# Seven-product form for half of the columns of a first matrix layer, and feature work given to either of two engines, in a fused attention and gated-layer kernel

## The chip, the cores and the metric

The kernel runs on one core of a Trainium2 chip. A core has five engines that run their own instruction streams beside each other: TensorE multiplies matrices (in the profile PE for the products and PEld for the loading of the stationary operand), VectorE (DVE) and ScalarE (ACT) do elementwise work, GpSimd (POOL) does small copies and issues some transfers, and SyncE (SP) issues the other transfers. An engine takes its instructions in the order in which they stand. The metric is the time of one execution in microseconds of device time; smaller is better. For the kernel before, the median of 11 runs is 292.11 us (291.77 to 294.96).

## What is computed

Two stages, one after the other, in float32 at the borders:

```python
# q, k, v: [8 batches, 8 heads, 576 positions, 64]
def phi(x, c, s):
    r = np.maximum(x, 0.0)
    return np.concatenate([r * c, r * s], axis=-1)
q_p, k_p = phi(q, cos_w, sin_w), phi(k, cos_w, sin_w)
kv  = np.einsum('bhsf,bhsd->bhfd', k_p, v)
num = np.einsum('bhsf,bhfd->bhsd', q_p, kv)
den = np.einsum('bhsf,bhf->bhs', q_p, k_p.sum(axis=2))[..., None] + 1e-06
x = (num / den).transpose(0, 2, 1, 3).reshape(4608, 512)
h = x @ w_in                  # w_in: [512, 2048]
g = h * np.cos(h)
out = g @ w_out               # w_out: [2048, 512], out: [4608, 512]
```

cos_w and sin_w depend on the position alone.

## The kernel before

The 4608 tokens are worked in nine chunks of 512. Chunks 0 to 7 are the first 512 positions of the eight batches; the last chunk (8) collects the 64 positions left over from each batch (tile xR in place of xT). Operands of the products are 16-bit floats, sums in PSUM are 32-bit.

**Attention of a batch.** Queries, keys and values are loaded in 32 bits into the tiles qm, km, vm. There is one such tile per name, so the next batch's load waits for the work that reads the present one. `prep` (lines 337 to 351) makes one of the two feature halves (cosine or sine) for one block of 128 tokens: relu and a scale per token, 128x512 values, written as 16 bits to kp or qp. `cast_v` (353 to 363) turns a block of v into 16 bits. From batch 2 on, `attention` (799 to 823) gives cosine halves and v casts to VectorE and sine halves to ScalarE. `kv` (365) multiplies keys and values on TensorE; `q_dma` and `x_dma` turn blocks round by transfers; `num` (419) makes numerator and denominator and has VectorE divide: an add, a reciprocal and a product (lines 450 to 454).

**First layer.** `layer1` (501 to 542) takes one chunk. From chunk 2 on it does 16 column blocks of 128, each as four products 128x128 by 128x512 that add up in one PSUM bank (line 539). Three banks M1 are used in turn. `gate` (491 to 499) then has ScalarE compute the cosine of the bank into a tile ch (as a sine with an offset, line 494) and VectorE multiply bank and ch into gT in 16 bits (line 496).

**Second layer.** From chunk 1 on `layer2` (609 to 693) splits g and w_out into 2x2 blocks and forms the four block results from seven block products in place of eight. The sums of blocks that this needs are made by VectorE: those of w_out once (`w_out_sums`, tiles T1 to T4, lines 595 to 607), those of g for each chunk (tiles S2, S3 and parts of gT in place, lines 625 and 670). Each product has two parts of eight matmuls 128x128 by 128x256 (line 643) in two banks M2 that go on adding while ScalarE (`copy`, 654) and VectorE (`plus`, 658) take out the running values into Y1, U2, Z5 and the output tiles ost.

**Order.** No loop sets the order of the instructions. Every call adds a step with an engine, a cost, a due time and the data that it reads and writes to a list (class `Plan`). `Plan.run` lays the list out by a forward pass (each engine takes the ready step with the smallest key) and a backward pass (which makes latest start times, the keys of the next forward pass), twelve times, and keeps the shortest. The instructions of every engine are then written in that order. So a change of one step's cost, engine or data can move others anywhere in the kernel.

Of the kernel before, what the change touches and what calls it, by code (L numbers as in the profile page):

```python
# [15 lines left out]

class Plan:


# [20 lines left out]
    def add(self, eng, occ, lat, due, fn, rd=(), wr=(), dma=None, lane=None):  # L40

        n = len(self.steps)
        prev = self.lanes.get(lane)
        if lane is not None:
            self.lanes[lane] = n
        deps = set()
        for key in rd:
            if key in self.wr:
                deps.add(self.wr[key])
        for key in wr:  # L50
            if key in self.wr:
                deps.add(self.wr[key])
            deps.update(self.rd.get(key, ()))
        for key in rd:
            self.rd.setdefault(key, []).append(n)
        for key in wr:
            self.wr[key] = n
            self.rd[key] = []
        deps.discard(n)
        self.steps.append(dict(eng=eng, occ=occ, lat=lat, due=due, fn=fn,  # L60
                               deps=deps, dma=dma, n=n, prev=prev))
        return n

    def run(self):


        key = [s["due"] for s in self.steps]
        best = None
        for _ in range(self.PASSES):
            start, done = self.forward(key)  # L70
            end = max(done)
            if best is None or end < best[0]:
                best = (end, start, done)
            key = self.backward(start, done, end)
        for s, a, b in zip(self.steps, best[1], best[2]):
            s["start"], s["end"] = a, b
        return sorted(self.steps, key=lambda s: (s["start"], s["n"]))

    def link(self, n, u):
        st = self.steps  # L80
        same = st[u]["eng"] == st[n]["eng"] and st[n]["dma"] is None
        return 0.0 if same else self.LINK[st[n]["eng"]]

    def forward(self, key):
# [9 lines left out]
        free = {e: 0.0 for e in self.LINK}  # L94
        ready = {e: [] for e in self.LINK}
        rings, now = {r: [] for r in self.SHARE}, 0.0
        for n, k in enumerate(left):
            if not k:
                ready[st[n]["eng"]].append(n)

        def release(n):
            for u in users[n]:
                avail[u] = max(avail[u], done[n] + self.link(n, u))
                left[u] -= 1
                if not left[u]:
                    ready[st[u]["eng"]].append(u)
        todo = len(st)
        while todo:
            best = None
            for e, cand in ready.items():  # L110
                if not cand:
                    continue
                limit = max(free[e], min(avail[n] for n in cand)) + self.PATIENCE.get(e, 0.0)
                k, t, n = min((key[n], max(free[e], avail[n]), n) for n in cand
                              if avail[n] <= limit)
                if best is None or t < best[0]:
                    best = (t, e, n)
# [23 lines left out]
            s = st[n]  # L141
            ready[e].remove(n)
            start[n] = t
            free[e] = t + s["occ"]
            if n in follow:
                u = follow[n]
                avail[u] = max(avail[u], t)
                left[u] -= 1
                if not left[u]:
                    ready[st[u]["eng"]].append(u)  # L150
            if s["dma"] is None:
# [53 lines left out]
def kernel(  # L205
# [41 lines left out]
    def sb(name, shape, dt=F16):  # L247
        return pool.tile(shape, dt, name=name)
# [4 lines left out]
    WARM = sb("WARM", [P, 1], F32)  # L253
    WZ = sb("WZ", [P, SM])
    w_in_sb = sb("w_in_sb", [P, NCT, Dff])
    w_out_sb = sb("w_out_sb", [P, NJT, Dm])
    V1 = sb("V1", [P, NT + 1, H, D1])
    JH, MH, TH = NJT // 2, Dm // 2, SM // 2
    T1, T2, T3, T4 = [sb(f"T{n}", [P, JH, MH]) for n in range(1, 5)]
    S2, S3 = [sb(f"S{n}", [P, JH, TH]) for n in (2, 3)]  # L260
    Y1, U2, Z5 = [sb(nm, [P, 2, MH], F32) for nm in ("Y1", "U2", "Z5")]
    raw = {nm: sb(f"{nm}m", [P, H, NT + 1, D], F32) for nm in "kqv"}
# [27 lines left out]

    Q_PE, X_PE = (), range(1, 3)
    ORDER0, ORDER1, HOLDW = "qkv", "kqv", 1
    GATE1 = (w_in_sb[0:2, 0, Dff // 2 + 1:Dff // 2 + 2], [("w_in", 2)])
# [14 lines left out]
    def act(occ, due, fn, rd, wr, lat=0.15):  # L308
        pl.add("ACT", occ, occ + lat, due, fn, rd, wr)


# [25 lines left out]
    def prep(b, nm, t, g, eng, due, hs=slice(0, H), after=()):  # L337
        dst = (kp if nm == "k" else qp)
        out_, in_ = dst[:, t, hs, g, :], raw[nm][:, hs, t, :]
        sc = CS[:, b % 2, g, t:t + 1]  # L340
        heads = range(H)[hs]
        rd = hk(nm, heads) + ["CS", *after]
        wr = [(nm + "p", t, g, h) for h in heads]
        f = len(heads) / H
        if eng == "ACT":
            act(0.12 + 0.5 * f, due, lambda: nc.scalar.activation(  # L346
                out=out_, in_=in_, func=AF.Relu, scale=sc), rd, wr)
        else:
            dve(0.09 + 0.33 * f, due, lambda: nc.vector.tensor_scalar(  # L349
                out=out_, in0=in_, scalar1=0.0, scalar2=sc,  # L350
                op0=ALU.max, op1=ALU.mult), rd, wr)

    def cast_v(b, t, eng, due, hs=slice(0, H)):
# [3 lines left out]
        f = len(heads) / H  # L357
        if eng == "ACT":
            act(0.12 + 0.5 * f, due, lambda: nc.scalar.activation(  # L359
                out=out_, in_=in_, func=AF.Copy), rd, wr)  # L360
        else:
            dve(0.09 + 0.33 * f, due, lambda: nc.vector.tensor_copy(  # L362
                out=out_, in_=in_), rd, wr)

# [136 lines left out]
    def layer1(c):  # L501
# [3 lines left out]
        if c < 2:  # L505
# [24 lines left out]
            return  # L530
        for n in range(NJT):
            j = n // 2 + (n % 2) * JH if c < B else n
            m = m1n[0] % NM1
            m1n[0] += 1
            due = start[c] + n * width[c] / NJT

            def mm(m=m, j=j):
                for cc in range(NCT):
                    nc.tensor.matmul(M1[m], lhsT=w_in_sb[:, cc, j * P:(j + 1) * P], rhs=X[:, cc, :],  # L539
                                     start=(cc == 0), stop=(cc == NCT - 1))  # L540
            pe(NCT, MM, due, mm, xk + [("w_in", j // 4)], [("M1", m)])
            gate(M1[m], ("M1", m), G[:, j, :], [("g", c % 2, j, t) for t in range(NT)], due + 1.5)

# [51 lines left out]
    def w_out_sums():  # L595
# [5 lines left out]
        def tt(out_, a, b, op, rd, wr):  # L601
            dve(1.14, start[2] - 8, lambda: nc.vector.tensor_tensor(
                out=out_, in0=a, in1=b, op=op), rd, wr)
        tt(T1, b12, b11, ALU.subtract, wk, ["T1"])
        tt(T3, b22, b12, ALU.subtract, wk, ["T3"])
        tt(T2, b22, T1, ALU.subtract, wk + ["T1"], ["T2"])
        tt(T4, b21, T2, ALU.subtract, wk + ["T2"], ["T4"])

    def layer2(c):
# [46 lines left out]

        def plus(dst, bank, other, ok, dk, due):
            dve(0.61, due, lambda: nc.vector.tensor_tensor(
                out=dst, in0=view(bank), in1=other, op=ALU.add), [("M2", bank), ok], dk)
        ol, oh = on[0] % NO, (on[0] + 1) % NO  # L660
        on[0] += 2
        m0, m1 = slice(0, MH), slice(MH, Dm)
        d = product(A, a11, W[:, lo, m0], gk(0, 0) + wk, True, False)
        copy(Y1, A, ["Y1"], d + 0.5)
        d = product(Bk, a12, W[:, hi, m0], gk(1, 0) + wk, True, True)
        plus(ost[ol][:, :, m0], Bk, Y1, "Y1", [("ost", ol, 0)], d + 0.5)
        for q_ in range(NG):
# [5 lines left out]
        d = product(A, S2, T2, sk["S2"] + ["T2"], False, False)  # L673
        copy(U2, A, ["U2"], d + 0.5)
        d = product(Bk, a21, T1, gk(0, 1) + ["T1"], True, False)
        copy(Z5, Bk, ["Z5"], d + 0.5)
        d = product(A, S3, T3, sk["S3"] + ["T3"], False, False)
        plus(ost[oh][:, :, m1], A, Z5, "Z5", [("ost", oh, 1)], d + 0.5)
        d = product(Bk, a12, W[:, hi, m1], gk(1, 0) + wk, False, True)
        plus(ost[ol][:, :, m1], Bk, U2, "U2", [("ost", ol, 1)], d + 0.5)  # L680
        store(c, 0, ol, d + 1.5)
# [14 lines left out]
    def setup():  # L696
        nc.gpsimd.memset(WZ, 0.5)
        nc.vector.memset(PIH, math.pi / 2.0)
# [100 lines left out]
    def attention(b):  # L799
# [3 lines left out]
        for t in range(NT + 1):  # L803
            for g in range(2):
                prep(b, "k", t, g, "DVE" if g == 0 else "ACT", T + 1.2 * t)
        for t in range(NT + 1):
            cast_v(b, t, "DVE", T + 6 + 0.4 * t)
        kv(b, T + 8)
        for t in range(NT + 1):
            due = T + 8 + 1.2 * t  # L810
            for g in range(2):
                prep(b, "q", t, g, "DVE" if g == 0 else "ACT", due)
            if b in Q_PE:
# [23 lines left out]
    for c in range(2, NC):  # L837
        if c < B:
            attention(c)
        layer2(c - 1)  # L840
        layer1(c)
# [36 lines left out]
```

## Time and profile before

| what | value |
|---|---|
| median of 11 runs | 292.11 us |
| profiled execution, own time | 293.9 us |
| its span, first to last instruction | 292.1 us |
| mean granted TensorE clock | 0.982 |
| PE busy | 278.6 us, 95% |
| PEld busy | 195.5 us, 67% |
| DVE busy | 239.4 us, 82% |
| ACT busy | 182.9 us, 63% |
| POOL busy | 8.7 us, 3% |
| HBM traffic over the span | 158 GB/s |

Busy is the time in which at least one instruction of an engine is on record. Instructions of one engine overlap at their ends: two gate products of VectorE that last 0.68 us each take 1.28 us together, so that a queue of them moves on every 0.60 us. The work of an engine in a stretch is therefore counted here by such steps from start to start. Waits are put down to the engine whose signal came last.

### The profile page before, as it was taken

What the parts mean: (1) busy time and instruction counts of PE and PEld (TensorE: products, weight loads), DVE (VectorE), ACT (ScalarE), POOL (GpSimd) and SP (SyncE); (2) the same over time, 40 slices, a digit from 0 to 9 for tenths busy, and PEclk for the clock granted to TensorE, in tenths of its full rate; (3) what the DMA queues carried; (4) which work ended last, traced back from release to release, by engine and by line L of the source; (5) the groups of instructions that cost most, each with busy time, mean ns of one, the idle gap of its engine ahead of it and who ended that gap; (6) DMA issues with size and microseconds to landing.
All of it is one profiled execution on the core that took longest, in us unless ns stands there. A gap on an engine that the chain in (4) does not pass through costs nothing.

```text
span 292.1 us, 6281 instructions
## 1 busy us (share of the span) xinstructions
PE 278.6 (95%) x2460; PEld 195.5 (67%) x2460; DVE 239.4 (82%) x486; ACT 182.9 (63%) x293; POOL 8.7 (3%) x21
## 2 busy tenths in 40 slices
PE   7768998999999999998999999999999999999993
PEld 2446866587976677566756766675668566666783
DVE  2965788999999999999998999999789948665741
ACT  2943899799967865867396759485543554645420
POOL 1502200000000000000000000000000000000000
PEclk9985999999999999999999999999999999999999
DMA  6999999799819996998899899944915000300304
GB/s 217 309 209 268 295 259 333 232 209 268 257 18 302 188 307 190 261 246 218 256 203 285 218 269 156 268 123 106 147 39 180 20 0 2 144 2 1 134 12 144
DMA packets 77565, 53.27 MB, mean 182 GB/s; under 512 B 46048, under 2 KB 75232, under 8 KB 77536
## 3 DMA queue, kind: packets, MB, share of 16 engines
q1 hardware_dynamic: 72592, 48.12, 63.2%
q0 software_dynamic: 4224, 4.19, 8.7%
q10 hardware_dynamic: 720, 0.57, 0.6%
q8 instruction: 19, 0.31, 0.4%
q14 instruction: 10, 0.08, 0.1%
HBM read 36.74 MB, written 9.44 MB: 158 GB/s over the span
## 4 chain that ended last, share of the span: by engine, by line
PE 84%; DMA 6%; ACT 5%; DVE 2%; issue 1%; POOL 0%; SPq 0%; ACTq 0%
PE M L643 33%; PE M L539 33%; PE M L521 9%; DMA w_in_sb<-in_moe_w_in_dram 3%; PE ATT L434 3%; DMA km<-in_k_dram 3%; PE ATT L373 2%; PE M L583 2%; ACT ch L494 2%; ACT qp L346 1%; PE TR L583 1%; DVE gT L496 1%; ACT kp L346 1%; ACT V L359 0%; PE M L474 0%
## 5 line engine op out<-in xcount | busy, mean ns | idle before, releaser
L494 ACT ACTIVATE ch<-M,PIH 128x512 f32<-128x512 f32 x144 | 98.3, 686 | 69.1 <-PE M L539 56.4
L496 DVE TENSOR_TENSOR gT<-M,ch 128x512 f16<-128x512 f32 x144 | 96.6, 685 | 26.8 <-ACT ch L494 25.3
L539 PE MATMUL M<-xT,w_in_sb 128*128 128x512 f16 x384 | 93.8, 379 | 0.0
L643 PEld LDWEIGHTS <-gT 128*128 128x128 f16 x640 | 62.0, 98 | 15.9 <-issue 1.0
L539 PEld LDWEIGHTS <-w_in_sb 128*128 128x128 f16 x448 | 42.4, 98 | 35.1
L643 PE MATMUL M<-w_out_sb,gT 128*128 128x256 f16 x384 | 46.5, 273 | 0.8 <-ACT ost L654 0.8
L521 PE MATMUL M<-xT,w_in_sb 128*128 128x256 f16 x256 | 33.8, 291 | 1.0 <-ACT xT L478 0.8
L643 PE MATMUL M<-T,S 128*128 128x256 f16 x256 | 32.4, 273 | 0.0
L643 PE MATMUL M<-T,gT 128*128 128x256 f16 x256 | 32.0, 273 | 0.0
L521 PEld LDWEIGHTS <-w_in_sb 128*128 128x128 f16 x256 | 26.2, 104 | 6.3 <-issue 1.6
L643 PEld LDWEIGHTS <-S 128*128 128x128 f16 x256 | 24.9, 98 | 7.4
L346 ACT ACTIVATE qp<-qm,CS 128x512 f16<-128x512 f32 x38 | 25.4, 714 | 4.0 <-DMA qm<-in_q_dram 4.0
L346 ACT ACTIVATE kp<-km,CS 128x512 f16<-128x512 f32 x39 | 26.7, 716 | 0.3 <-DMA km<-in_k_dram 0.3
L454 DVE TENSOR_TENSOR x<-ATT,rec 128x512 f16<-128x512 f32 x33 | 22.8, 691 | 1.1
L349 DVE TENSOR_SCALAR qp<-qm,CS 128x512 f16<-128x512 f32 x42 | 18.6, 479 | 4.6 <-DMA qm<-in_q_dram 4.6
L625 DVE TENSOR_TENSOR S<-gT 128x1024 f16<-128x1024 f16 x32 | 21.5, 684 | 0.3
L349 DVE TENSOR_SCALAR kp<-km,CS 128x512 f16<-128x512 f32 x41 | 18.6, 487 | 0.4 <-DMA km<-in_k_dram 0.4
L434 PEld LDWEIGHTS <-qT 128*128 128x128 f16 x320 | 14.9, 98 | 5.9 <-issue 1.5
L539 PE MATMUL M<-xR,w_in_sb 128*128 128x512 f16 x64 | 16.1, 379 | 0.0
L434 PE MATMUL ATT<-kvz,qT 128*128 128x65 f16 x296 | 14.9, 194 | 0.8 <-DVE x L454 0.8
L373 PEld LDWEIGHTS <-kp 128*128 128x128 f16 x320 | 11.6, 97 | 3.5 <-ACT V L359 1.3
L362 DVE CAST V<-vm 128x512 f16<-128x512 f32 (+1 forms) x42 | 13.9, 391 | 0.0
(66 smaller groups left out, 181.6 us busy)
## 6 DMA issues: line engine op xcount, KB each, us to landing
out_dram<-ost SPq DMA_DIRECT2D x33, 256.0 KB, 3.6
qm<-in_q_dram SPq DMA_DIRECT2D x8, 640.0 KB, 6.4
km<-in_k_dram SPq DMA_DIRECT2D x8, 640.0 KB, 6.5
qm<-in_q_dram SPq DMA_DIRECT2D x8, 512.0 KB, 5.3
km<-in_k_dram SPq DMA_DIRECT2D x8, 512.0 KB, 5.6
vm<-in_v_dram SPq DMA_DIRECT2D x6, 640.0 KB, 5.5
vm<-in_v_dram SPq DMA_DIRECT2D x6, 512.0 KB, 6.0
w_in_sb<-in_moe_w_in_dram POOLq DMA_DIRECT2D x4, 512.0 KB, 9.5
```

The source lines that it names most:

```text
L346: act(0.12 + 0.5 * f, due, lambda: nc.scalar.activation(out=out_, in_=in_, func=AF.Relu, scale=sc), rd, wr)
L349: dve(0.09 + 0.33 * f, due, lambda: nc.vector.tensor_scalar(out=out_, in0=in_, scalar1=0.0, scalar2=sc, op0=ALU.max, op1=ALU.mult), rd, wr)
L362: dve(0.09 + 0.33 * f, due, lambda: nc.vector.tensor_copy(out=out_, in_=in_), rd, wr)
L373: nc.tensor.matmul(bank[hb][:, hh * D1:(hh + 1) * D1], lhsT=kp[:, t, h].rearrange("p g d -> p (g d)"), rhs=V1[:, t, h, :], start=(t == 0), ...
L434: nc.tensor.matmul(bank[hb][:, hh * D1:(hh + 1) * D1], lhsT=a[:, h, :], rhs=z[:, h, :], start=(i == 0), stop=(i == len(parts) - 1))
L454: nc.vector.tensor_tensor(out=split(x16[n][:, hs, :], k), in0=A[:, :, :, 0:D], in1=split(rec[n][:, hs], k).unsqueeze(3).broadcast_to((P, k ...
L494: act(0.59, due, lambda: nc.scalar.activation(out=ch[c], in_=bank, func=AF.Sin, bias=PIH, scale=1.0), [key, "PIH"], [("ch", c)])
L496: dve(0.61, due, lambda: nc.vector.tensor_tensor(out=dst, in0=bank if len(dst.shape) == 2 else bank.rearrange("p (j s) -> p j s", j=dst.sh ...
L521: nc.tensor.matmul(M1[m][:, jj * 2 * P:(jj + 1) * 2 * P], lhsT=w_in_sb[:, cc, j * P:(j + 1) * P], rhs=X[:, cc, ts], start=(cc == 0), stop= ...
L539: nc.tensor.matmul(M1[m], lhsT=w_in_sb[:, cc, j * P:(j + 1) * P], rhs=X[:, cc, :], start=(cc == 0), stop=(cc == NCT - 1))
L625: dve(0.07 + 1.07 / NG, due, lambda: nc.vector.tensor_tensor(out=out_[:, sl], in0=a[:, sl], in1=b[:, sl], op=op), rd, wr)
L643: nc.tensor.matmul(M2[bank][:, tt * MH:(tt + 1) * MH], lhsT=a[:, j, tt * P:(tt + 1) * P], rhs=b[:, j, :], start=(first and tt == 0 and j = ...
```

## The change

1. In chunks 4 to 8, half of the 16 column blocks of the first layer are made in the seven-product form that the second layer already uses. Two groups of four column blocks (two of the lower and two of the upper half of the columns) are done with `layer1_fast`; the other eight blocks stay as they were (`layer1_plain`).
2. The sums that this needs: three new tiles and one in place for parts of w_in, made once (`w_in_sums`), and four sums of the chunk's xT or xR, made for each chunk (`layer1_sums`). The running values of a group are taken out of PSUM by three copies on ScalarE and three sums on VectorE into 32-bit tiles, and three of the four gates of a group read these tiles; the fourth reads PSUM. From chunk 7 on, tiles that held q, k and v serve as further sets of these.
3. Room is made: T1 is written over the part of w_out that it was made from; Y1, U2 and Z5 go, and `layer2` takes its running values out into the output tiles; the tile of the warm-up products is a part of S2.
4. The first layer has four PSUM banks in turn from chunk 3 on (TR is the fourth), three before.
5. The planner takes steps that either of several engines can do. It puts such a step on the engine on which its forward pass ends it sooner. `attention` uses this for both feature halves and for the v casts: VectorE or ScalarE. Batches 0 and 1 keep their engines.

```diff
     def link(self, n, u):
         st = self.steps
-        same = st[u]["eng"] == st[n]["eng"] and st[n]["dma"] is None
+        same = st[u]["eng"] == st[n]["eng"] and st[n]["dma"] is None and len(st[u]["opts"]) == 1
         return 0.0 if same else self.LINK[st[n]["eng"]]
...
+        def first(n, e, t):
+            opts = st[n]["opts"]
+            return len(opts) == 1 or all(
+                t + opts[e][1] <= max(free[x], avail[n]) + o[1] for x, o in opts.items())
...
-    T1, T2, T3, T4 = [sb(f"T{n}", [P, JH, MH]) for n in range(1, 5)]
+    T1 = w_out_sb[:, 0:JH, MH:Dm]
+    T2, T3, T4 = [sb(f"T{n}", [P, JH, MH]) for n in range(2, 5)]
...
-    Y1, U2, Z5 = [sb(nm, [P, 2, MH], F32) for nm in ("Y1", "U2", "Z5")]
+    WZ = S2[:, 0:2, :].rearrange("p j s -> p (j s)")
...
+    VCAST = ("DVE", "ACT")
...
+        cost = {"DVE": 0.09 + 0.33 * f, "ACT": 0.12 + 0.5 * f}
...
+        either(due, {e: c for e, c in cost.items() if eng in (e, "")}, fn, rd, wr)
...
+        for g in range(NJT // 4):
+            if g < nf:
+                layer1_fast(c, g, X, xk)
+            if g < len(todo):
+                for j in [2 * todo[g] + i + JH * hf for i in range(2) for hf in range(2)]:
+                    layer1_plain(c, j, X, xk)
+
+    def next_bank(c):
+        nb = 4 if c > 2 else NM1
+        m1n[0] += 1
+        return BANKS[m1n[0] % nb]
...
+    FAST1 = {c: 2 for c in range(4, NC)}
...
+    def w_in_sums(f, due):
...
+        tt(3, a11, a21, ALU.subtract, [], gone["k"])
+        tt(1, a21, a22, ALU.add, [], gone["q"] if f else [("w_in", 2)])
+        tt(2, ws[1], a11, ALU.subtract, [("WS", 1, f)], [])
+        tt(4, a12, ws[2], ALU.subtract, [("WS", 2, f)], [])
...
+    def layer1_sums(c, X, xk):
...
+        tt(0, b12, b11, [], (hk("k") + hk("q") + hk("v") + ["AL"]) if c == B - 1 else ())
+        tt(2, b22, b12, [])
+        tt(1, b22, XS[0], [("XS", i, 0)])
+        tt(3, b21, XS[1], [("XS", i, 1)])
...
+    def layer1_fast(c, g, X, xk):
...
+            def mm():
+                for j in range(2):
+                    for cc in range(CH2):
+                        nc.tensor.matmul(
+                            bank[0][:, j * TH:(j + 1) * TH], lhsT=a(cc, j), rhs=b[:, cc, :],
...
+        d = product(A, -11, b11, xk, True, False)
+        copy(Y, A, zk[0], d)
+        d = product(Bk, -12, b21, xk, True, True)
+        plus(Y, Bk, zk[0], d)
+        out(Y, zk[0], 0, 0, d)
+        d = product(A, 2, XS[1], [("XS", i, 1)], False, False)
+        copy(U, A, zk[1], d)
+        d = product(Bk, 1, XS[0], [("XS", i, 0)], True, False)
+        copy(Z, Bk, zk[2], d)
+        d = product(A, 3, XS[2], [("XS", i, 2)], False, False)
+        plus(Z, A, zk[2], d)
+        out(Z, zk[2], 1, 1, d)
+        d = product(Bk, 4, b22, xk, False, True)
+        plus(U, Bk, zk[1], d)
+        out(U, zk[1], 0, 1, d)
+        d = product(A, -22, XS[3], [("XS", i, 3)], False, True)
+        out(A[0], A[1], 1, 0, d)
...
-        copy(Y1, A, ["Y1"], d + 0.5)
+        copy(ost[ol][:, :, m0], A, [("ost", ol, 0)], d + 0.5)
...
-        plus(ost[ol][:, :, m0], Bk, Y1, "Y1", [("ost", ol, 0)], d + 0.5)
+        plus(ost[ol][:, :, m0], Bk, ("ost", ol, 0), d + 0.5)
...
-                prep(b, "k", t, g, "DVE" if g == 0 else "ACT", T + 1.2 * t)
+                prep(b, "k", t, g, "", T + 1.2 * t)
...
-            cast_v(b, t, "DVE", T + 6 + 0.4 * t)
+            cast_v(b, t, "", T + 6 + 0.4 * t)
...
-                prep(b, "q", t, g, "DVE" if g == 0 else "ACT", due)
+                prep(b, "q", t, g, "", due)
...
+        if c == SUMS_AT + 1:
+            w_in_sums(0, start[c] - 12)
...
```

Here `product` makes one block product of a group (four matmuls), `copy`, `plus` and `out` are the copy on ScalarE, the sum on VectorE and the gate; `tt` is one sum of two tiles on VectorE, and `either` adds a step with several engines to the list.

## Prediction

> **What bounds the kernel now.** First the slices of the span: busy tenths of each engine in 40 equal pieces, then the chain of waits by engine, then the same chain piece by piece in time (start, length, what).
>
> ```profile
> PE   7768998999999999998999999999999999999993
> DVE  2965788999999999999998999999789948665741
> ACT  2943899799967865867396759485543554645420
> PE 84%; DMA 6%; ACT 5%; DVE 2%; issue 1%; POOL 0%; SPq 0%; ACTq 0%
> ...
> 145.72 2.59 PE M L539 x12
> 275.43 12.24 PE M L643 x112
> ```
>
> TensorE is on the chain for 84% of the span, and from the ninth slice (58 us) on it is never idle for long. The chain also gives the true price of a product, since a piece runs from start to start: 2.59 us / 12 = 0.2158 us for 128x512 (layer 1), 12.24 / 112 = 0.1093 us for 128x256. (The rows of groups say 379 and 273 ns; those are durations that overlap.)
>
> Next the stretches between the bursts of layer 2 that open a chunk: length, then busy time and count of PE, PEld, DVE, ACT.
>
> ```profile
> 110.00:137.40 27.40, 26.60 (x234) 17.79 (x232) 26.15 (x56) 18.80 (x32) 0.00 (x0) 1.00 0.93 228
> 137.40:166.30 28.90, 28.90 (x266) 20.05 (x266) 27.20 (x57) 18.84 (x31) 0.00 (x0) 1.00 0.99 237
> 166.30:194.60 28.30, 28.30 (x251) 19.47 (x249) 26.50 (x57) 20.24 (x33) 0.00 (x0) 1.00 0.93 211
> 194.60:223.30 28.70, 28.70 (x266) 19.88 (x265) 25.19 (x50) 14.36 (x23) 0.00 (x0) 1.00 0.55 121
> 223.30:250.00 26.70, 26.70 (x182) 17.52 (x179) 20.79 (x35) 13.72 (x21) 0.00 (x0) 1.00 0.13 45
> ```
>
> The second to fifth are chunks 4 to 7 with layer 2 of the chunk before; chunk 8 takes 25.4 us (250.0 to 275.4). TensorE fills them. VectorE is the near second to about 200 us (26 to 27 of 28), ScalarE has a third free. The one stretch where PE is short is looked at in the order of time:
>
> ```profile
> 134.34 1.94 ACT L346 ACTIVATE qp<-qm,CS 128x512 f16<-128x512 f32 x3
> 136.75 0.59 ACT L654 ACTIVATE ost<-M 128x512 f32<-128x512 f32 x1
> 137.38 3.65 PE L643 MATMUL M<-w_out_sb,gT 128*128 128x256 f16 x32 [0.80 <-ACT ost L654]
> ```
>
> Three features stand on ScalarE ahead of a gate and of the copy that empties a bank; TensorE, done with its last piece at 136.4, starts again at 137.38: 0.92 us lost. I find no other gap of PE above 0.3 us after 60 us.
>
> **The change, part by part.** The sum is made against the profiled execution, 293.9 us with a span of 292.1; the median is 1.8 us lower, and I shift the result by that.
>
> *Products (on the path).* A plain group of four column blocks is 16 x 0.2158 = 3.45 us; a fast one is seven products of four, 28 x 0.1093 = 3.06. Two groups in five chunks: 10 x 0.39 = **3.9 us saved**, 0.8 per chunk. [...] The pieces of the chain, 216 and 109 ns with a weight load before each product, decide: weight loads (98 ns, beside the products) stay hidden at 256 columns, as they do in layer 2.
>
> *VectorE.* Steps from start to start: two gates 1.28 us, so 0.60; kp to the next instruction 0.40 (192.75 to 193.15); three v casts 1.09, so 0.34; 128x1024 in 16 bits 0.60. Added: 30 sums from PSUM (the row of L658 is the same form) x 0.61 = 18.3; 4 sums of w_in x 0.61 = 2.4; 20 sums of xT, 128x512 in 16 bits. This form has no row; by the line through 128x1024 (0.68) and 128x2048 (1.21) it is 0.42, its step 0.34 (0.20 if it scaled with nothing fixed, 0.60 if it cost as much as the larger one): 6.7, ends 4 and 12. Moved away, by the order in which the built instructions stand: 18 query and 7 key halves x 0.40 and 19 v casts x 0.34 = 16.5. Net +10.9 us. Gates stay 144 in number; those that read the new 32-bit tiles (30) I take at the same 0.60.
>
> *ScalarE.* 25 halves x 0.61 and 19 casts x 0.55 (between 0.41 for 128x256 and 0.71 for a half) = 25.7, and 30 copies x 0.48 = 14.4: +40 us.
>
> Counting each chunk's instructions by these steps, from its predecessor's last gate to its own:
>
> | chunk | PE before, after | DVE before, after | ACT before, after |
> |---|---|---|---|
> | 4 | 28.9, 28.1 | 27.6, 28.0 | 18.5, 25.5 |
> | 5 | 28.3, 27.5 | 26.5, 26.1 | 19.2, 25.0 |
> | 6 | 28.7, 27.9 | 23.9, 25.3 | 11.9, 20.2 |
> | 7 | 26.7, 25.9 | 18.4, 23.2 | 10.9, 13.8 |
> | 8 | 25.4, 24.6 | 16.2, 20.7 | 11.9, 14.3 |
>
> Chunks 2 and 3 fall by 0.5 and 0.9 on VectorE, so over chunks 2 to 6 it has 129.6 us both before and after: the moves pay for the sums, and the rest lands in chunks 7 and 8, where cover is 2.7 and 3.9 us. The work fits under PE, but chunk 4 with nothing to spare. [...]
>
> *Chains inside a group.* Two banks alternate; each product waits for the bank's evacuation, about 0.17 to signal plus 0.6 to 0.7. Seven products and six evacuations need some 5 us, twice per chunk, and layer 2 and the plain blocks give PE some 20 us of other work, which the new order does put between them. Cost by this cover 0; without it, 10 groups x up to 0.92 us (the gap above, the nearest row). A gain of its own is excluded, since a chain can only hold PE. I take two such gaps in all, **1.8 us**, because VectorE's idle time between 80 and 197 us was 4 us and PE's share of it shrinks.
>
> *The old gap at 136.4.* The order there is new and a fourth bank gives one more gate's time (0.86 us) of room: **0.9 us saved**, 0 if the same queue forms again.
>
> *Edits with one answer.* The first w_in sum is put early, between the third and fourth normalisation of batch 0, and waits for two parts of w_in; the later landed at 20.5 and VectorE then stood idle from 19.9 to 22.9 us anyway. With a late landing it would delay the fourth block and the start of layer 1 one for one. T1 in place, the shared tiles and ost as scratch add no instruction; ost's reuse is some 15 us after its store was issued, stores land in 3.6. SyncE issues as many transfers as before (87 and 53 transposes), but features that ScalarE finishes later let the next loads start later; after 80 us nothing waited for a transfer, so cost 0, or what a late load (6.5 us to land) shows beyond its lead.
>
> *End.* The last 112 products stand after the last gate as before; between them and the last layer-1 product now lie two parts of chunk 7 (1.75 us), and by steps the sums S2 and S3 are ready some 0.4 us before their turn. Tail unchanged.
>
> Sum: 293.9 - 3.9 - 0.9 + 1.8 = 290.9; less 1.8 for the median, **289.1 us**.
>
> **Rivals.**
> *A, the forecast* (0.58): PE still bounds, 287.3 (no new gap) to 290.6.
> *B, ScalarE's queue holds PE, slower* (0.17). From chunk 3 on the old order has two runs of three or more features or casts in a row on ScalarE, of which one made the gap; the new has eight, most where chunks change over and a bank waits to be emptied. If each costs 0.92: 292.1 - 4.8 + 7.4 = 294.7. It decides from 5.3 such stalls. For it: the same pattern, more often, and ScalarE at 25 of 28 us. Against: the fourth bank, and the other old run that cost nothing.
> *C, the saving is eaten* (0.20): VectorE, with no slack in chunks 4 and 5, hands each group's bank back 0.4 us late: 10 x 0.4 = 4, so 291.3, no measurable change. For it: 28.0 against 28.1; against: the backlog can wait on four banks and drain in chunks 7 and 8.
> *D* (0.05): the re-planned start (chunks 0 to 2) or late loads shift everything by 2 us or more, either way, about 292 at the mean.
>
> **How the numbers follow.** The likeliest is A. Its bottom, 287.3, is no stall at all; above, B beyond its middle is left out, so the range is 287.2 to 292.9. Half a per cent is 1.46 us, about what a measurement of this kernel can tell from no change. Faster: A and a part of C and D, 0.66; within it 0.17; slower 0.17.
>
> **What would show it.** Right: layer-1 products of 256 columns at 0.109 us in the chain, PE at 9 in all slices, VectorE's slices 9 to the end of chunk 6 and higher than before in 7 and 8, the last product some 3 us earlier. Wrong: waits of PE on ScalarE copies or on features in front of them (B), on VectorE sums of the new tiles (C), on transfers after 80 us (D), or pieces of 256 columns slower than 0.109.

## The result, and the profile after

The changed kernel takes 288.89 us (median of 12 runs, 287.23 to 291.02) against 292.35 us before (median of 47 runs, 291.52 to 294.96). The ratio is given as 0.9872, 95% interval [0.9848, 0.9896], 1.3% faster; it is not the quotient of the two medians, which is 0.988. The forecast was 289.1 us. A later measurement of the same kernel on another occasion (below) gave 290.26 against 292.32 us and 0.9919 [0.9889, 0.9949]. So the saving is 3.5 us in one and 2.1 us in the other; 0.99 is as much as both support, and a third decimal is not to be leaned on.

The page of the profiled execution of the changed kernel: slices, the chain by engine, and the waits of TensorE from 56 us on (the table of waits for that stretch; engine and line, what it waited for, us in total, times, longest).

```profile
PE   8668999899999999999999999999999999999993
DVE  2976878999999998979989999999899999978931
ACT  2945897999999998769979999998764477567320
PE 73%; DMA 12%; ACT 6%; DVE 5%; issue 2%; SPq 1%; ACTq 0%; DVEq 0%
...
PE M L815 <- ACT ost L826: 0.4, 1, 0.4
```

TensorE's row has lost its dip in the middle. VectorE's nines, with some eights and sevens between them, now reach to the 35th slice, ScalarE's to the 27th. One wait of TensorE on another engine is left after 56 us. The new thing stands in the chain: transfers hold 12% of it, 6% before.

The same stretches as before, cut at the bursts of layer 2 (columns as in the prediction):

```profile
136.20:163.20 27.00, 26.97 (x250) 21.17 (x250) 25.66 (x52) 24.77 (x43) 0.00 (x0) 1.00 1.13 248
163.20:190.70 27.50, 27.50 (x279) 21.81 (x276) 26.70 (x55) 26.70 (x46) 0.00 (x0) 1.00 0.79 157
190.70:218.70 28.00, 28.00 (x291) 22.31 (x288) 26.17 (x51) 21.33 (x36) 0.00 (x0) 1.00 0.45 97
218.70:243.00 24.30, 24.30 (x192) 18.58 (x191) 23.29 (x43) 15.34 (x26) 0.00 (x0) 1.00 0.14 50
243.00:267.60 24.60, 24.60 (x197) 18.99 (x195) 21.51 (x37) 15.52 (x26) 0.00 (x0) 1.00 0.11 43
```

The last two cuts are not at the same work as before, so the lines are not compared one by one; what they show is that TensorE is without a pause in all five while VectorE and ScalarE fill up to 26.7 of 27.5 us.

**Where the 5.9 us of the span came from.** The span fell from 292.1 to 286.2 us, more than the medians did. Four common points of TensorE's timeline divide it. The same 80 products of chunk 0 (start, length), before and then after:

```profile
25.74 10.76 PE L521 MATMUL M<-xT,w_in_sb 128*128 128x256 f16 x80 [0.84 <-ACT xT L478]
```

```profile
25.27 8.89 PE L546 MATMUL M<-xT,w_in_sb 128*128 128x256 f16 x80 [0.87 <-ACT xT L503]
```

They took 1.9 us less with nothing changed in them. The granted clock stands third from the right in the windows from 15 to 30 us, before and then after:

```profile
15.00:30.00 15.00, 11.85 (x102) 8.25 (x102) 8.09 (x25) 6.10 (x10) 2.40 (x7) 0.66 1.19 240
15.00:30.00 15.00, 11.96 (x126) 9.31 (x125) 10.76 (x30) 7.83 (x13) 2.39 (x7) 0.89 1.20 240
```

That the change does not set it is seen from the version with the form from chunk 3 on (`from_3`, below): one of its profiles has 0.66 in this stretch, the other 1.00. At the first long run of chunk 1's products (58.36 and 56.35) the lead is 2.0 us; the slower products of chunk 0 account for nearly all of it. From there to the burst that opens chunk 4 (137.38, then 136.23, where the new order has also done the 1.21 us of one batch's key-value products) it gains 0.35 us. From that burst to the last product (285.74, then 279.65) it gains 3.73 us, with those 1.21 us put back. That last stretch is what the prediction calls the products: 3.9 us, less a gap of 0.2 us at 237.5. Nor do the medians have all of the 5.9 us: the profiled execution before was 1.6 us above its median, the one after 0.9 us below its own.

### The profile page after: what moved, and what is told of

It is laid out like the page before. It is cut to its first block, busy times and chain, and to the rows that moved or that the text cites. A ratio compares the mean times of both kernels' runs of the same rounds, so it can differ in the third digit from the quotient of the medians.

```text
span 286.2 us, 6553 instructions
## 1 busy us (share of the span) xinstructions
PE 272.7 (95%) x2580; PEld 206.3 (72%) x2580; DVE 247.9 (87%) x496; ACT 219.2 (77%) x367; POOL 8.8 (3%) x21
## 4 chain that ended last, share of the span: by engine, by line
PE 73%; DMA 12%; ACT 6%; DVE 5%; issue 2%; SPq 1%; ACTq 0%; DVEq 0%
PE M L815 29%; PE M L578 14%; PE M L678 8%; DMA vm<-in_v_dram 7%; PE M L546 7%; PE TR L678 3%; PE TR L578 3%; DMA km<-in_k_dram 3%; DMA qm<-in_q_dram 3%; PE ATT L459 3%; ACT qp L374 2%; ACT ch L519 2%; PE M L755 2%; PE ATT L398 2%; DVE x L479 1%
## 5 line engine op out<-in xcount | busy, mean ns | idle before, releaser
L519 ACT ACTIVATE ch<-M,PIH 128x512 f32<-128x512 f32 x95 | 63.8, 685 | 14.6 <-PE M L578 7.5
L521 DVE TENSOR_TENSOR gT<-M,ch 128x512 f16<-128x512 f32 x95 | 63.7, 683 | 7.0 <-ACT ch L519 6.6
L815 PE MATMUL M<-w_out_sb,gT 128*128 128x256 f16 x512 | 62.1, 272 | 0.4 <-ACT ost L826 0.4
L578 PE MATMUL M<-xT,w_in_sb 128*128 128x512 f16 x208 | 51.1, 379 | 0.0
L374 ACT ACTIVATE qp<-qm,CS 128x512 f16<-128x512 f32 x56 | 38.0, 720 | 6.5 <-DMA qm<-in_q_dram 6.5
L374 ACT ACTIVATE kp<-km,CS 128x512 f16<-128x512 f32 x46 | 31.0, 716 | 2.6 <-DMA km<-in_k_dram 2.1
L826 ACT ACTIVATE ost<-M 128x512 f32<-128x512 f32 x31 | 18.5, 597 | 11.9 <-PE M L815 11.6
L830 DVE TENSOR_TENSOR ost<-M,ost 128x512 f32<-128x512 f32 x24 | 16.4, 682 | 5.7 <-issue 3.3
L519 ACT ACTIVATE ch<-Z,PIH 128x512 f32<-128x512 f32 x21 | 14.9, 716 | 2.1 <-DVE Z L690 2.0
L519 ACT ACTIVATE ch<-TR,PIH 128x512 f32<-128x512 f32 x19 | 13.1, 687 | 3.9 <-PE TR L578 2.7
```

The costliest lines, as they stand in the source:

```text
L374: fn = {"ACT": lambda: nc.scalar.activation(out=out_, in_=in_, func=AF.Relu, scale=sc), "DVE": lambda: nc.vector.tensor_scalar(out=out_, i ...
L519: act(0.59, due, lambda: nc.scalar.activation(out=ch[c], in_=bank, func=AF.Sin, bias=PIH, scale=1.0), [key, "PIH"], [("ch", c)])
L521: dve(0.61, due, lambda: nc.vector.tensor_tensor(out=dst, in0=bank if len(dst.shape) == 2 else bank.rearrange("p (j s) -> p j s", j=dst.sh ...
L578: nc.tensor.matmul(M, lhsT=w_in_sb[:, cc, j * P:(j + 1) * P], rhs=X[:, cc, :], start=(cc == 0), stop=(cc == NCT - 1))
L815: nc.tensor.matmul(M2[bank][:, tt * MH:(tt + 1) * MH], lhsT=a[:, j, tt * P:(tt + 1) * P], rhs=b[:, j, :], start=(first and tt == 0 and j = ...
L826: act(0.5, due, lambda: nc.scalar.activation(out=dst, in_=view(bank), func=AF.Copy), [("M2", bank)], dk)
```

## The experiments

Ratios are to the kernel before, measured beside each version on one chip. The last three columns are from the profiles, one execution each. "Start" is when the first long run of chunk 1's products begins, "main part" the time from there to the start of the last product, and "no product" the part of it that is left when the products in it are taken off at their steps in these traces (0.2158 us for 512 columns, 0.109 for 256, 0.056 for 128, 0.030 for 65). So the start, where the granted clock differs from execution to execution (0.66 to 1.00 in the mean from 15 to 30 us), is kept apart from the part that the change touches. All in us.

| version | median | ratio, 95% interval | start | main part | no product |
|---|---|---|---|---|---|
| before | 292.35 | 1 | 58.4 | 229.0 | 1.5 |
| changed | 288.89 | 0.9872 [0.9848, 0.9896] | 56.4 | 224.9 | 1.1 |
| choice_only | 292.1 | 0.9981 [0.9954, 1.0007] | 56.6 | 229.0 | 0.9 |
| one_group | 290.87 | 0.9918 [0.9888, 0.9947] | 57.5 | 226.5 | 0.4 |
| no_plus | 288.57 | 0.9856 [0.9818, 0.9893] | 57.1 | 225.0 | 0.9 |
| fast_only | 299.37 | 1.021 [1.016, 1.0259] | 54.8 | 236.5 | 11.1 |
| v_on_dve | 290.31 | 0.9909 [0.9875, 0.9942] | 58.8 | 225.1 | 1.5 |
| three_banks | 289.36 | 0.9915 [0.9884, 0.9945] | 57.3 | 225.5 | 1.5 |
| from_3 | 288.12 | 0.9851 [0.9819, 0.9883] | 58.5 | 224.2 | 0.9 |
| all_in_last | 292.27 | 0.9987 [0.9957, 1.0017] | 58.7 | 226.8 | 3.5 |
| casts_free | 291.55 | 0.9956 [0.9922, 0.9989] | 56.4 | 228.8 | 3.5 |
| changed_again | 290.26 | 0.9919 [0.9889, 0.9949] | 56.9 | 225.6 | 1.7 |
| from_3_again | 288.37 | 0.9853 [0.9822, 0.9883] | 57.8 | 224.2 | 0.9 |
| from_2 | 290.08 | 0.9909 [0.9878, 0.9941] | 58.2 | 225.9 | 3.7 |

The changed kernel's own ratio moved from 0.9872 to 0.9919 between two occasions. Of the others, only casts_free, from_3_again and from_2 were measured together with it (the second time), so a difference of half a per cent between other rows says little, and the profiles have to decide.

### How much of the gain is products

```diff
-    FAST1 = {c: 2 for c in range(4, NC)}
-    SUMS_AT = min(FAST1) - 1
+    FAST1 = {}
+    SUMS_AT = NC
```

> Seven-product groups of the first layer taken out (all 16 column blocks plain in every chunk); the free choice of engine, four banks and shared tiles stay. Theory (TensorE bounds, the gain is the 3.9 us of products): TensorE has all its old work, so 291.6 to 292.4, ratio to before 0.997 to 1.000, with VectorE's busy time some 15 us lower and no effect of that. Rival (the gain came from relief of VectorE and ScalarE by the free choice): 289 to 290.5, ratio 0.988 to 0.994.

Measured 0.9981, no change that can be told. Without the seven-product groups VectorE is relieved (230.1 us busy, 239.4 before) and TensorE waits for nothing above 0.6 us after 56 us, but it has its old work, and the main part takes the 229.0 us that it took before. Relief of the other engines alone is worth next to nothing here.

```diff
-    FAST1 = {c: 2 for c in range(4, NC)}
+    FAST1 = {c: 1 for c in range(4, NC)}
```

> One seven-product group per chunk from chunk 4 on, in place of two. Theory (each group saves its 0.39 us and nothing is given back): 5 x 0.39 = 1.95 us of the 3.9, ratio halfway between 0.9872 and 1, about 0.993, 290.4. Rival (the first group pays and the second is eaten by VectorE, or the other way round): near 0.987 or near 1.000.

(In this version the plain blocks 10 and 11 of chunks 4 to 8 are multiplied with the sums that now lie in their place.) Measured 0.9918. The medians cannot tell a half: 292.1, 290.87 and 288.89 us for none, one and two groups, but 290.26 for two on the other occasion. In the profiles the main part falls by 2.5 us with the first group of each chunk and by 1.6 or 0.9 us with the second. The products removed are the same 2.0 us each time; the difference is in the time without a product (0.9, 0.4, then 1.1 or 1.7 us). So each group brings what its products save, and the second gives a part of it back. An exact half is not shown.

### Whether VectorE holds TensorE back

```diff
-            dve(0.61, due + 0.3, lambda: nc.vector.tensor_tensor(
-                out=dst, in0=bank[0], in1=dst, op=ALU.add), [bank[1], key], [key])
+            dve(0.09, due + 0.3, lambda: nc.vector.tensor_tensor(
+                out=dst[:, 0:8], in0=bank[0][:, 0:8], in1=dst[:, 0:8], op=ALU.add), [bank[1], key], [key])
```

> The 30 sums of a fast group on VectorE cut from 512 to 8 columns each, which leaves most of three of the four block results of each group incomplete: some 15 us less work on VectorE in chunks 4 to 8, products unchanged. Theory (TensorE bounds there, stalls are below 0.7 us in all): at most 0.5 us faster than the changed kernel, ratio 0.985 to 0.988. Rival (VectorE, full in chunks 4 and 5, holds TensorE back): 1.5 us or more faster, ratio below 0.982.

Measured 0.9856, inside the interval of the changed kernel. VectorE's busy time fell from 247.9 to 237.2 us, less than the 15 us that were meant, since the planner gave some features back to it. The main part is 225.0 us, 224.9 and 225.6 in the two profiles of the changed kernel. What these sums cost VectorE costs the changed kernel no time that could be told.

```diff
-                prep(b, "k", t, g, "", T + 1.2 * t)
+                prep(b, "k", t, g, "DVE" if g == 0 else "ACT", T + 1.2 * t)
...
-            cast_v(b, t, "", T + 6 + 0.4 * t)
+            cast_v(b, t, "DVE", T + 6 + 0.4 * t)
...
-                prep(b, "q", t, g, "", due)
+                prep(b, "q", t, g, "DVE" if g == 0 else "ACT", due)
```

> The seven-product groups with the old engines: cosine halves and v casts of batches 2 to 7 on VectorE, sine halves on ScalarE. Theory (the free choice is what makes room on VectorE): VectorE needs about 32, 31.5 and 29 us in chunks 4 to 6 where TensorE needs 28, so some 6 to 9 us are lost against the changed kernel: 295 to 298, ratio 1.01 to 1.02, with TensorE waiting for gates in chunks 4 to 6. Rival (banks and later chunks absorb the load): 289 to 290, ratio 0.987 to 0.992.

Measured 299.37, 2% slower than before and worse than expected. The windows of this version over chunks 5 and 6, and one of its gaps in the timeline of TensorE and of VectorE:

```profile
165.00:196.60 31.60, 28.87 (x268) 21.89 (x266) 30.70 (x66) 22.07 (x38) 0.00 (x0) 0.95 0.88 204
196.60:225.00 28.40, 25.15 (x249) 19.78 (x247) 28.16 (x59) 16.45 (x28) 0.00 (x0) 1.00 0.49 103
```

```profile
164.33 0.93 PE L815 MATMUL M<-w_out_sb,gT 128*128 128x256 f16 x7
167.32 1.92 PE L815 MATMUL M<-w_out_sb,gT 128*128 128x256 f16 x12 [2.06 <-DVE gT L521]
```

```profile
165.19 0.69 DVE L830 TENSOR_TENSOR ost<-M,ost 128x512 f32<-128x512 f32 x1
165.79 0.88 DVE L375 TENSOR_SCALAR kp<-km,CS 128x512 f16<-128x512 f32 x2
166.57 0.69 DVE L521 TENSOR_TENSOR gT<-TR,ch 128x512 f16<-128x512 f32 x1
```

VectorE is the engine without a pause (28.16 of 28.40 us), TensorE waits. At 165 us layer 2 needs a gate of chunk 4, and that gate stands on VectorE behind a sum and two key features. From 134 us on TensorE has seven gaps, 1.0 to 2.3 us long from start to start, which make 8.5 us, less the 0.16 us between starts that I count as no gap. Two end with a gate of VectorE (3.7 us of waiting), three with a sum of VectorE (2.2), two with a copy of ScalarE (1.5). The clock has a part, too: its mean is 0.95 in the first window shown and 1.00 in the second; 5% of 31.6 us makes another 1.6 us in this execution, by estimate. So the products pay only because features and casts leave VectorE: with one part of the change the kernel is slower, with the other it is unchanged, with both faster.

Two versions give back one class of steps each: only the feature halves go back to their old engines, or only the casts go back to VectorE.

```diff
-                prep(b, "k", t, g, "", T + 1.2 * t)
+                prep(b, "k", t, g, "DVE" if g == 0 else "ACT", T + 1.2 * t)
...
-                prep(b, "q", t, g, "", due)
+                prep(b, "q", t, g, "DVE" if g == 0 else "ACT", due)
```

> The changed kernel with the feature halves on their old engines; the v casts of batches 2 to 7 may go to either. By steps VectorE then needs 28.3, 29.5 and 28.1 us in chunks 4 to 6 where TensorE needs 28.1, 27.5 and 27.9. Theory (the time follows VectorE's excess, 2.4 us in all, as it did with both classes on their old engines): 290.5 to 292, ratio 0.993 to 0.999. Rival (the casts alone make room enough): 288.5 to 289.5, ratio 0.986 to 0.990.

Measured 0.9956, as the theory had it, though its interval overlaps with that of the changed kernel on the same occasion. The profile is clearer: TensorE is 3.5 us without a product after the start, 1.1 and 1.7 in the changed kernel. Most of its gaps are in 164 to 201 us, where by steps VectorE's work is above TensorE's; the two largest, near 192 us, end with a copy of ScalarE (0.7 us of waiting) and a gate of VectorE (0.8).

```diff
-    VCAST = ("DVE", "ACT")
+    VCAST = ("DVE",)
```

> The changed kernel with the v casts of batches 2 to 7 on VectorE alone; the feature halves still go to either engine. Theory (what matters is that VectorE's sum fits under TensorE, whichever step moves): the planner moves more feature halves instead, VectorE stays at 26 to 28 us in chunks 4 to 6, so at most 0.7 us slower than the changed kernel, ratio 0.986 to 0.990. Rival (the casts are what had to go): 290.5 or more, ratio above 0.993.

Measured 0.9909, just outside the range of the theory and not in that of the rival; with an interval of 0.7% it decides nothing. The profile speaks for the theory: the main part is 225.1 us with 1.5 us without a product, as in the changed kernel, with one larger gap, 0.7 us of waiting for a copy of ScalarE at 192 us. What is later is the start, 58.8 us, with a loss of another kind at 51 to 57 us (a mean clock of 0.79 from 50 to 58 us, see the last section).

### The fourth bank

```diff
-        nb = 4 if c > 2 else NM1
+        nb = NM1
```

> The changed kernel with three banks in turn for the first layer in every chunk; two of the three alternate in a fast group. Theory of the prediction (the fourth bank gives the room that removes the old gap of 0.9 us): TensorE loses 0.5 to 1.5 us in gaps, 289.5 to 290.5, ratio 0.990 to 0.994. Rival (the gap in the changed kernel is still there with four banks, 0.47 us, behind the copy of an output block, so banks of the first layer have no part in it): ratio as for the changed kernel, 0.986 to 0.989.

The ratio (0.9915) lies in the theory's range, its interval reaches into the rival's, and the changed kernel itself gave 0.9919 the second time, so it decides nothing. The traces say more. With three banks there is no gap of TensorE near 136 us at all; its one gap above 0.3 us is at 269.8, where it waits 0.7 us for the copy of an output block, which has no part in the banks of layer 1. With four banks (the changed kernel, first profile) the old gap is still there:

```profile
134.93 0.76 ACT L374 ACTIVATE qp<-qm,CS 128x512 f16<-128x512 f32 x1
135.55 0.63 ACT L826 ACTIVATE ost<-M 128x512 f32<-128x512 f32 x1
```

```profile
136.23 1.03 PE L815 MATMUL M<-w_out_sb,gT 128*128 128x256 f16 x8 [0.44 <-ACT ost L826]
```

TensorE again waits for the same copy behind a query feature. In the second profile of the changed kernel, with the same order and the same four banks, the gap is not there. So four banks do not remove it and three do not bring it; what differs between the two profiles is when ScalarE's queue got going (below). The main part is no longer with three banks (225.5 us) than with four (224.9 and 225.6).

### How far the form can be taken

```diff
-    FAST1 = {c: 2 for c in range(4, NC)}
+    FAST1 = {c: 2 for c in range(3, NC)}
```

> Seven-product groups from chunk 3 on, in place of 4: two more groups. Theory (TensorE bounds as long as VectorE and ScalarE fit): another 2 x 0.39 = 0.8 us of products saved, but by steps VectorE needs 28.6 us in chunk 5 and ScalarE 28.6, where TensorE needs 27.5, so one to two us come back as gaps of TensorE in chunks 4 and 5: 288.5 to 290, ratio 0.987 to 0.993. Rival (there is still room): 288.1, ratio 0.9845.

The rival was right: 288.12. Beside the changed kernel on one chip:

> The changed kernel, unaltered, beside the two versions with more groups. 288.9 us as before, ratio 0.985 to 0.990.

> Groups from chunk 3 on, once more, beside the changed kernel on one chip. Theory (two groups more save 0.8 us and cost no gap): 0.5 to 1.0 us faster than the changed kernel, ratio 0.983 to 0.987. Rival (its first result was chance): the same as the changed kernel or slower.

288.37 against 290.26 us, ratios 0.9853 and 0.9919. In both measurements this version's median is below the changed kernel's, by 0.8 and 1.9 us; as the changed kernel's two medians lie 1.4 us apart, the size of the lead is open. In the profiles the main part is 224.2 us twice, against 224.9 and 225.6. One step further:

```diff
-    FAST1 = {c: 2 for c in range(4, NC)}
+    FAST1 = {c: 2 for c in range(2, NC)}
```

> Seven-product groups from chunk 2 on. Theory (products save 0.39 us a group until VectorE and ScalarE together are full): four groups more than the changed kernel, 1.6 us less for TensorE, but by steps VectorE needs 29.0 us in chunk 3 and ScalarE 33.8 in chunk 1 and 29.1 in chunk 3, where TensorE needs about 27.5, so at least 1.5 us come back: 288.5 to 291, ratio 0.986 to 0.995, and no better than starting from chunk 3. Rival (room is still left): 287.3, ratio 0.982.

Measured 0.9909: 1.7 us slower than from chunk 3 on, measured together, as expected. TensorE is 3.7 us without a product after the start, 0.9 from chunk 3 on. It waits 1.1 us for a gate of VectorE at 133.6 us and has smaller gaps. The last try filled the last chunk:

```diff
-    FAST1 = {c: 2 for c in range(4, NC)}
+    FAST1 = {c: 2 if c < NC - 1 else 4 for c in range(4, NC)}
```

> All four groups of the last chunk in the seven-product form, two in chunks 4 to 7. Theory: 0.8 us less for TensorE; VectorE needs 25.2 us in the last chunk where TensorE needs 23.8, and the second set of sums of w_in makes 2.4 us more, so 0 to 1.5 us come back as a wait between the last gates and layer 2: 288.1 to 289.5, ratio 0.984 to 0.990. Rival (VectorE's excess stands on the path in full, with the chains of groups that have no plain blocks between them): 290 or more, ratio above 0.992.

No better than before (0.9987). The wait that was expected at the end is there:

```profile
275.62 0.60 PE L815 MATMUL M<-T,S 128*128 128x256 f16 x4
277.30 0.94 PE L815 MATMUL M<-T,S 128*128 128x256 f16 x7 [1.08 <-DVE S L797]
```

It is about a third of the 4.0 us by which this span is longer than that of the changed kernel. The larger part is at the start, where the planner, given another list, put other steps first: TensorE waits 3.6 us for VectorE's divisions between 48 and 53 us, then runs at a lower clock (a mean of 0.79 from 50 to 58 us, last section), and the first long run of chunk 1 starts at 58.7 us, 56.4 in the changed kernel. So this run does not say what the form costs in the last chunk alone.

## Why the prediction was right, step by step

*The number, 289.1 us: nearer than the method allows.* The forecast saved 3.0 us; 3.5 and 2.1 were measured. That the first came within 0.2 us of the forecast is luck, since the median of the same kernel moved by 1.4 us, and in the first profile two of the three terms were too large, a saving and a cost (below). The mechanism and the largest term are what held.

*Products, 3.9 us: right.* The chain of the changed kernel has pieces of eight 256-column products of layer 1 at 0.87 us (0.109 each), and from the opening of chunk 4 to the last product 3.73 us are gained. The weight loads of these products, 98 ns each, stay beside them.

*VectorE and ScalarE by steps: right.* The sums of xT, for which there was no row, follow each other in 0.34 us, the value taken:

```profile
142.68 0.42 DVE L637 TENSOR_TENSOR XS<-xT,XS 128x512 f16<-128x512 f16 x1
143.02 0.41 DVE L637 TENSOR_TENSOR XS<-xT 128x512 f16<-128x512 f16 x1
143.36 0.42 DVE L637 TENSOR_TENSOR XS<-xT,XS 128x512 f16<-128x512 f16 x1
```

Gates that read the 32-bit tiles take VectorE 682 ns (683 from PSUM) and ScalarE 716 (685), on ScalarE 0.03 us more than was counted. A queue of VectorE still moves on every 0.60 us (four gate products and the start of the sum behind them, 149.46 to 151.86 us), the step that was counted. That VectorE fits, and only just, is what fast_only, casts_free and from_2 show from the other side.

*New gaps, 1.8 us: too high, and wrong in place.* The first profile has one new gap, 0.21 us at 237.5, and 0.47 us left of the old one at 135.6; the second profile of the same kernel has 1.10 at 152.9 and the same 0.21. They were ascribed to chains inside a group and to VectorE's lost slack. The two larger ones come from the term that was set to nothing, the later loads. The chain of the second profile (start, us, what), then ScalarE's timeline there:

```profile
145.48 6.72 DMA qm<-in_q_dram
...
152.91 0.67 ACT ch L519
153.58 0.50 ACT Z L686
154.08 0.04 issue
154.12 0.60 PE TR L678 x4
```

```profile
149.56 1.30 ACT L519 ACTIVATE ch<-M,PIH 128x512 f32<-128x512 f32 x2
152.29 0.72 ACT L374 ACTIVATE qp<-qm,CS 128x512 f16<-128x512 f32 x1 [1.43 <-DMA qm<-in_q_dram]
```

A query feature that now stands in ScalarE's queue waits 1.43 us for its load; behind it are a gate and the copy that a fast group's next product needs, and TensorE stops 1.07 us. In the first profile the same wait on the same kind of load is 2.28 us long at 121.5, and the chain runs from it through features and gates to the copy at 135.55 and the gap after it. Before the change nothing waited for a transfer after 60 us, which was read as a reason to set the term to nothing. That the features had stood later against their loads then is the likely reason; it was not tried. The version from chunk 3 on has no wait for a load after 60 us in either profile, and its largest gap there is 0.24 us; that it owes the rest of its lead to this was not tried by itself.

*The old gap, 0.9 us saved: right in size in one profile, half in the other, for the wrong reason.* 0.92 became 0.47 in the first profile and nothing in the second. The reason given, the fourth bank, fails: with three banks the gap is gone as well.

*The first w_in sum: no cost, as said.* It ran at 19.95 us without a wait, in the pause of VectorE, so in this execution its parts of w_in had landed before the 20.5 us that were read from the profile before.

*Rivals.* B (ScalarE's queue): in these two profiles the runs of three features cost TensorE nothing by themselves; a feature that waits 1.43 us for its load does (TensorE stops 1.07 us). C (VectorE): the place is right, as fast_only shows, but the free choice of engine keeps the changed kernel short of it. D's late loads are the mechanism that did show, at 0.5 and 1.1 us in place of the 2 us or more given there.

## What to carry to other kernels

Here an exchange of TensorE work for VectorE work gave 288.89 us where VectorE had room (26.70 of 27.50 us busy at most) and 299.37 where it had none (28.16 of 28.40), against 292.35 before; so count the work of each engine per stage by steps from start to start, and see whether other steps can leave the one that fills. When such steps move to another engine's queue, ask what each of them waits for: here a feature that waited 1.43 us for its load held the gate and the copy behind it, and TensorE stopped 1.07 us, though nothing had waited for a load after 60 us before the change. With a planner, a small edit can move the start of the kernel by more than it is worth; look at the first stretch before the stage that was edited.

## What was not expected of the hardware

The granted clock of TensorE in the start differs between executions. From 15 to 30 us its mean was 0.66 before and 0.89 after, worth 1.9 us over 80 products. The version from chunk 3 on had 0.66 in its first profile; in its second it had 1.00, but 0.83 from 5 to 15 us. That second one, with v_on_dve, from_2 and all_in_last, shows a mean of 0.79 from 50 to 58 us, where the others have 1.00. In all four TensorE had just stood idle for 1.6 to 2.6 us in one wait, for VectorE's divisions or a copy of ScalarE. In fast_only twelve products of 256 columns behind a wait of 2.06 us for a gate, at 167.3 us, took 1.92 us, 1.47 in the changed kernel (at 238.7). Eight products of 512 columns behind one of the four waits took 3.27 us in place of 1.89:

```profile
51.98 0.42 PE L459 MATMUL ATT<-kvz,qT 128*128 128x65 f16 x8 [1.99 <-DVE x L479]
52.24 0.38 PE L499 MATMUL M<-IDENT,x 128*128 128x128 f16 x4
52.46 3.27 PE L755 MATMUL M<-w_out_sb,gT 128*128 128x512 f16 x8
```

(the version from chunk 3 on, second profile). But no_plus stood idle for 2.12 us before 53.2 and had no such stretch (1.00 from 50 to 58 us), nor is there one in fast_only behind its second wait for a gate, some 1.6 us of the 3.7: the only slices of its page with a clock below 9 are the one from 162.8 to 170.2 us, around the first wait, and the last. So an idle time of that length alone does not bring it about; what else does was not tried.
